# Summing the last six rows of a weight matrix in four rows of 256 columns in two PSUM banks, with the final copy on two engines

## Chip, cores, metric

One core of one Trainium2 chip. The metric is device microseconds of the whole program. All timed runs quoted here are fast: none is more than 1.5% above the fastest of its kernel. A comparison is given as the ratio of the mean of one kernel's fast runs to the mean of the other's of the same rounds, with a 95% interval, so it is not quite the ratio of the medians that stand beside it.

## The reference, cut to what matters

A decode step for one token: grouped-query attention over a cache of 65536 keys, plus an MLP, both added to the input.

```python
x = A_x                                   # (1, 1, 1024)
xn = _layernorm(x)
# A: q = xn @ wq ; softmax(q k^T) v over 4 kv heads x 65536 keys ; @ wo (4096 x 1024)
# B: ... h2 = gelu(layernorm(x1) @ w3) @ w4          w4 is 3584 x 1024
return x + A(xn, k_cache, v_cache, wq, wo) + B(xn, w1, w2, w3, w4)
```

The output is one row of 1024 values. 170 MB of weights and cache are read for it.

## The kernel before

Everything that ends in the output row is accumulated in one tile `psB` of PSUM (the memory into which TensorE writes its sums) as two rows of 512 columns (`j` = 0, 1), each in its own 32-column group of the TensorE array, so that the two matmuls of a row run side by side. The weight w4 is the last thing to be loaded, in eight pieces of 6, 5, 6, 4, 3, 2, 1 and 1 rows; a row here is `hT[:, c]` (128 values) times 128 x 1024 weights. "Row 27" below is the last one.

```python
W4_PIECES = (6, 5, 6, 4, 3, 2, 1, 1)
...
ps_S = ...  # bufs=1, 4 banks     ps_O: 1 bank     ps_M: 2 banks     ps_B: 1 bank  (all eight in use)
psB = ps_B.tile([P, 512], F32, name="psB")

def row_acc(j, lhsT, rhs, start=False):
    nc.tensor.matmul(psB[32 * j:32 * j + 32, :], lhsT=lhsT.to_broadcast([lhsT.shape[0], 32]), rhs=rhs, start=start,
                     stop=False, tile_position=(0, 32 * j), skip_group_check=True)
...
def compute_w4(lo, hi):
    wt = st.tiles["w4"]
    for c in range(lo, hi):
        for j in range(2):
            row_acc(j, hT[:, c:c + 1], wt[:, D * c + 512 * j:D * c + 512 * (j + 1)])
...
compute_k(NU - 1)
tail["rows"] = ps_S.tile([P, SUBS, 512], F32, name="o_acc", tag="sc")
for g in range(HKV - 1):
    project(g)                      # 48 matmuls with wo
add_projection()                    # o_rows: fp32 rows added into psB by two fp32 matmuls
compute_v(NU - 1)
early = sum(W4_PIECES[:2])
compute_w4(0, early)
project(HKV - 1)
compute_w4(early, FC)

out_t = ogpool.tile([64, 512], BF16, name="out_t", tag="og")
nc.scalar.copy(out=out_t[:], in_=psB[0:64, :])
nc.scalar.dma_start(out=out[0, 0, :].rearrange("(j n) -> j n", j=2), in_=out_t[31:33, :])
```

All 32 partitions of a quadrant hold the same row, so partitions 31 and 32 are the two rows of the output, next to each other.

## Time and profile before

| | before |
|---|---|
| median time | 401.06 us (400.98 to 401.21, 3 runs) |
| span of the profile | 398.9 us |
| DMA engines busy | 0.9 or more in nearly every slice, 426 GB/s |
| last load (row 27 of w4) landed | 396.52 |
| its two matmuls start | 396.56 |
| copy out of PSUM (ScalarE) | 396.99, 0.58 us |
| output DMA issued | 397.60, that is 1.08 us after the landing |

The chain of waits that ended last in the kernel before, its last five pieces (start us, us, what):

```profile
379.12 17.39 DMA big<-in_B_w_dram
396.52 0.04 issue
396.56 0.41 PE psB L221 x2
396.97 0.02 issue
396.99 0.58 ACT out_t L485
```

Up to 396.52 the chain is loads alone. Only the last 0.41 + 0.58 us are work that this change can shorten. The timeline of the same microseconds (start us, us, engine, line, operation, tiles, shapes, count, and in brackets the idle time before it and what ended it):

```profile
396.56 0.39 PE L221 MATMUL psB<-big,hT 128*32 128x512 bf16 x2 [0.25 <-DMA big<-in_B_w_dram]
...
396.99 0.58 ACT L485 CAST out_t<-psB 64x512 bf16<-64x512 f32 x1 [29.44 <-PE psB L221]
397.60 0.26 ACTq L486 DMA_DIRECT2D out_dram<-out_t  x1
```

TensorE sat idle 0.25 us for the last row: its backlog had just cleared.

### The profile page before, as it was taken

To read this page: it belongs to the slowest core of one execution; us is meant where nothing else is said; L and a number is where in the kernel's file an instruction comes from. 1 tells how busy PE (TensorE), PEld (TensorE's weight loads), DVE (VectorE), ACT (ScalarE), POOL (GpSimd) and SP (SyncE) were. 2 spreads that over 40 slices of the span, in tenths; PEclk is the share of its full clock that TensorE was granted. 3 is DMA by queue.
4 is the path that set the end of the run, shared out by engine and by line. 5 is a ranking of instruction groups with operands and counts; after the bars stand their busy time and mean duration, and the time that the engine had idled before them with its cause. 6 is when DMAs were issued, how large, how long until landed. Compare 5 with 4: busy or idle time off the path is not lost.

```text
span 398.9 us, 2547 instructions
## 1 busy us (share of the span) xinstructions
PE 232.8 (58%) x1348; PEld 45.1 (11%) x854; DVE 209.0 (52%) x154; ACT 27.3 (7%) x35; POOL 5.3 (1%) x28
## 2 busy tenths in 40 slices
PE   0571970591479238742974196539462945494987
PEld 0210000010100110010101010200020101010133
DVE  0601010964196569634953895269439942884130
ACT  1001010003000200020002000200100011002000
POOL 2000000000000000000000000000000000000000
PEclk9995996596869687956795889569855997698889
DMA  9998999999999999999999999999999999999996
GB/s 421 421 454 369 440 447 486 421 427 421 416 435 421 427 493 416 427 427 427 435 421 421 486 421 427 422 427 434 434 422 460 434 427 389 424 457 447 390 418 258
DMA packets 4575, 170.01 MB, mean 426 GB/s; under 512 B 467, under 2 KB 469, under 8 KB 982
## 3 DMA queue, kind: packets, MB, share of 16 engines
q1 hardware_dynamic: 4560, 169.87, 98.9%
q8 instruction: 8, 0.13, 0.1%
q14 instruction: 1, 0.01, 0.0%
q10 hardware_dynamic: 6, 0.00, 0.0%
HBM read 169.87 MB, written 0.00 MB: 426 GB/s over the span
## 4 chain that ended last, share of the span: by engine, by line
DMA 58%; DVE 20%; PE 18%; ACT 2%; issue 1%; DVEq 0%; ACTq 0%
DMA big<-in_A_k_cache_dram 34%; DVE big L357 14%; DMA big<-in_B_w_dram 14%; DMA big<-in_A_v_cache_dram 11%; PE sc L362 7%; PE oacc L412 5%; PE psh L287 3%; DVE p_sb L383 2%; DVE mx L367 2%; ACT p_sb L380 2%; PE ps L334 1%; PE psB L221 1%; PE pm_mx L369 0%; DVE m L371 0%; DVE ol L432 0%
## 5 line engine op out<-in xcount | busy, mean ns | idle before, releaser
L362 PE MATMUL sc<-big,qdiag 128*128 128x512 bf16 x512 | 128.5, 411 | 66.3 <-DVE big L357 66.1
L357 DVE STREAM_TRANSPOSE big<-big 128x4096 f32<-128x4096 f32 x32 | 139.4, 4413 | 50.1 <-DMA big<-in_A_k_cache_dram 50.1
L412 PE MATMUL oacc<-big,p_sb 128*32 128x512 bf16 x512 | 43.9, 511 | 34.5 <-DVE p_sb L383 34.5
L367 DVE TENSOR_REDUCE mx<-sc 128x1 f32<-128x2048 f32 x8 | 18.3, 2292 | 29.8 <-PE sc L362 29.8
L362 PEld LDWEIGHTS <-qdiag 128*128 128x128 bf16 x128 | 13.1, 103 | 177.1 <-issue 145.1
L380 ACT ACTIVATE p_sb<-sc,nball 128x2048 bf16<-128x2048 f32 x8 | 15.7, 1967 | 219.8 <-DVE nball L378 219.8
L383 DVE STREAM_TRANSPOSE p_sb<-p_sb 128x2048 bf16<-128x2048 bf16 x8 | 18.5, 2311 | 18.0 <-ACT p_sb L380 18.0
L412 PEld LDWEIGHTS <-p_sb 128*32 128x32 bf16 x512 | 16.5, 124 | 58.6 <-DVE p_sb L383 35.1
L287 PE MATMUL psh<-big,ln_rep_b 128*32 128x512 bf16 (+1 forms) x64 | 12.8, 968 | 7.5 <-DMA big<-in_B_w_dram 7.5
L451 PE MATMUL o_acc<-big,oT 128*1 128x512 bf16 x48 | 13.0, 440 | 2.4 <-ACT p_sb L380 2.4
L369 PE MATMUL pm_mx<-ident_f,mx 128*1 128x128 f32 x8 | 2.4, 295 | 19.1 <-DVE mx L367 19.1
L326 DVE STREAM_TRANSPOSE h_row<-h_row 128x896 bf16<-128x896 bf16 x1 | 1.1, 1112 | 21.0 <-ACT h_row L325 21.0
L421 DVE SCALAR_TENSOR_TENSOR og<-oacc,wb,og 128x512 f32<-128x512 f32 x4 | 3.0, 746 | 15.7 <-PE oacc L412 15.7
L221 PE MATMUL psB<-big,hT 128*32 128x512 bf16 x56 | 8.3, 430 | 0.3 <-DMA big<-in_B_w_dram 0.3
L457 DVE COPY o_rows<-o_acc 1x1024 f32<-1x1024 f32 x1 | 1.2, 1212 | 13.8 <-PE oacc L412 13.8
L235 PE MATMUL pm_ln<-ln_rowsum_a,ones_f 128*128 128x1 f32 x2 | 0.6, 347 | 12.6 <-DVE ln_rowsum_a L233 12.6
L433 PE MATMUL pm_e<-ol,sel8big 128*128 128x129 f32 x8 | 2.6, 414 | 7.9 <-DVE ol L432 7.9
L287 PE MATMUL psq<-big,ln_rep_a 128*32 128x512 bf16 x64 | 6.4, 585 | 1.3 <-DMA big<-in_A_wq_dram 1.3
L311 POOL COPY qdiag<-qx 32x32 bf16<-32x32 bf16 x16 | 3.2, 203 | 279.1 <-PE sc L362 249.1
L226 DVE STREAM_TRANSPOSE x_t<-x_row 32x256 bf16<-32x256 bf16 x4 | 2.5, 616 | 8.2 <-DMA x_row<-in_A_x_dram 8.1
L299 DVE CAST q_row<-psq 128x512 bf16<-128x512 f32 x1 | 0.7, 692 | 8.4 <-PE psq L287 8.4
L376 PE MATMUL pm_mx<-ident_f,rep 1*128 1x1 f32 x8 | 1.9, 240 | 5.0 <-DVE rep L373 5.0
(95 smaller groups left out, 73.6 us busy)
## 6 DMA issues: line engine op xcount, KB each, us to landing
big<-in_A_wo_dram SPq DMA_DIRECT2D x1, 8192.0 KB, 35.9
big<-in_B_w_dram SPq DMA_DIRECT2D x1, 7168.0 KB, 38.2
big<-in_B_w_dram SPq DMA_DIRECT2D x2, 2048.0 KB, 46.0
big<-in_B_w_dram SPq DMA_DIRECT2D x2, 1536.0 KB, 27.2
big<-in_B_w_dram SPq DMA_DIRECT2D x1, 1280.0 KB, 23.9
big<-in_B_w_dram SPq DMA_DIRECT2D x1, 1024.0 KB
big<-in_B_w_dram SPq DMA_DIRECT2D x1, 768.0 KB, 30.6
big<-in_B_w_dram SPq DMA_DIRECT2D x1, 512.0 KB, 31.4
```

What stands on the lines that cost most here:

```text
L221: nc.tensor.matmul(psB[32 * j:32 * j + 32, :], lhsT=lhsT.to_broadcast([lhsT.shape[0], 32]), rhs=rhs, start=start, stop=False, tile_positio ...
L287: nc.tensor.matmul(acc[32 * q:32 * q + 32, i, 0:n], lhsT=rep[:, c, :], rhs=cols(c, i, q), start=(c == 0), stop=(c == DC - 1), tile_positio ...
L311: nc.gpsimd.tensor_copy(out=qdiag[at, LEAD:].rearrange("p (x c) -> p x c", x=4)[:, :, 32 * a:32 * a + 8], in_=qx[at, :, 8 * g:8 * g + 8])
L334: nc.tensor.matmul(ps1[0:32, q, :], lhsT=xn2_rep[:, c, :], rhs=wt[:, 0, c, 512 * q:512 * (q + 1)], start=(c == 0), stop=(c == DC - 1), til ...
L357: nc.vector.transpose(out=words, in_=words)
L362: nc.tensor.matmul(sc[:, e, :], lhsT=qdiag[:, c0:c0 + P], rhs=cols[:, s, e, :, b2, :, r], start=(s == 0 and b2 == 0 and r == 0), stop=(s = ...
L367: nc.vector.reduce_max(out=mx[:], in_=sc[:].rearrange("p e n -> p (e n)"), axis=AX.X)
L380: nc.scalar.activation(out=p_sb[:], in_=sc[:], func=ACTF.Exp, bias=nball[:, b:b + 1], scale=SCALE, accum_out=group["lall"][:, b:b + 1])
L383: nc.vector.transpose(out=flat, in_=flat)
L412: nc.tensor.matmul(oacc[32 * q:32 * (q + 1), :], lhsT=pT[:, e, 32 * t:32 * (t + 1)], rhs=vt[:, :, e, t, :], start=(e == 0 and t < 4), stop ...
L421: nc.vector.scalar_tensor_tensor(out=og[:], in0=oacc[:], scalar=wb[:, 1:2], in1=og[:], op0=ALU.mult, op1=ALU.add)
L451: nc.tensor.matmul(tail["rows"][0:1, h2, :], lhsT=oT[g][:, j:j + 1], rhs=wt[:, g, j, 512 * h2:512 * (h2 + 1)], start=(g == 0 and j == 0), ...
```

## The change

Intent: make the work after the last landing shorter. The last six rows are summed in four rows of 256 columns, one per column group, in two PSUM banks, so that a row streams 256 columns instead of 512 and two engines can copy 256 columns each out of different banks at the same time. The sums up to row 21 stay in `psB`; they are copied to SBUF (`sums`) and added by four fp32 matmuls after three narrow rows (`AHEAD`). I call that copy and addition the handover.

```diff
--- before.py
+++ after.py
@@ -19,6 +19,8 @@
 SETS = 4
 SLOTS = 3
 W4_PIECES = (6, 5, 6, 4, 3, 2, 1, 1)
+NARROW = 6
+AHEAD = 3
 
 
 def keep_loaded_weights(nc):
@@ -479,12 +481,35 @@
     early = sum(W4_PIECES[:2])
     compute_w4(0, early)
     project(HKV - 1)
-    compute_w4(early, FC)
-
-    out_t = ogpool.tile([64, 512], BF16, name="out_t", tag="og")
-    nc.scalar.copy(out=out_t[:], in_=psB[0:64, :])
+    compute_w4(early, FC - NARROW)
+    sums = ogpool.tile([64, 512], F32, name="sums", tag="og")
+    nc.scalar.copy(out=sums[:], in_=psB[0:64, :])
+    quarters = [ps_M.tile([P, 512], F32, name="pm_r", tag="pm") for _ in range(2)]
+
+    def quarter_acc(lhsT, rhs, start=False):
+        for h in range(2):
+            for j in range(2):
+                q = 2 * h + j
+                nc.tensor.matmul(quarters[h][32 * q:32 * q + 32, 0:256], lhsT=lhsT(j), rhs=rhs(j, h), start=start, stop=False,
+                                 tile_position=(0, 32 * q), skip_group_check=True)
+
+    def narrow_rows(lo, hi, start=False):
+        wt = st.tiles["w4"]
+        for c in range(lo, hi):
+            quarter_acc(lambda j: hT[:, c:c + 1].to_broadcast([P, 32]),
+                        lambda j, h: wt[:, D * c + 512 * j + 256 * h:D * c + 512 * j + 256 * (h + 1)],
+                        start=start and c == lo)
+
+    narrow_rows(FC - NARROW, FC - NARROW + AHEAD, start=True)
+    quarter_acc(lambda j: ident_f[0:64, 32 * j:32 * j + 1].to_broadcast([64, 32]),
+                lambda j, h: sums[:, 256 * h:256 * (h + 1)])
+    narrow_rows(FC - NARROW + AHEAD, FC)
+
+    out_t = ogpool.tile([64, 2, 256], BF16, name="out_t", tag="og")
+    nc.scalar.copy(out=out_t[:, 0, :], in_=quarters[0][0:64, 0:256])
+    nc.vector.tensor_copy(out=out_t[:, 1, :], in_=quarters[1][64:128, 0:256])
     nc.scalar.dma_start(out=out[0, 0, :].rearrange("(j n) -> j n", j=2),
-                        in_=out_t[31:33, :])
+                        in_=out_t[31:33].rearrange("p h n -> p (h n)"))
 
 # ---- launch: one core; inputs and outputs as the reference has them ----
 _INS = ['A_x', 'A_k_cache', 'A_v_cache', 'A_wq', 'A_wo', 'B_x', 'B_w1', 'B_w2', 'B_w3', 'B_w4']
```

## The prediction

> **What bounds the kernel now.** By the page's slices the DMA engines are busy at 0.9 or more in nearly all of the span (398.9 us, 426 GB/s). The chain of waits of the last 60 us is nothing but loads: the V cache to 379.1, then w4 to 396.52, and after that only 0.41 us of TensorE (two matmuls of the last w4 row), 0.58 us of ScalarE (copy of 64x512 sums out of PSUM) and the output's DMA, issued at 397.60. The loads don't depend on anything the change touches, so only what follows 396.52 can gain: 0.41 + 0.58 us, 0.25% of the time.
>
> **What the change does, by the timeline and the trace's single instructions.**
> - Last row: two matmuls of 512 columns (0.39 us each, starting 3 ns apart) become four of 256 in four column groups. In the V stage four column groups already run at the pace of one matmul per 0.216 us each (starts a few ns apart, durations 0.38 to 0.39), so four abreast cost no more than two. The clock is at full speed from 389.5 to 399.7, where 512 columns stream in 0.213 us: 256 fewer save 0.107. Estimate: 0.39 becomes 0.28. This agrees with the Trainium skill, "TensorEngine Tiling (Array Packing)", Key Properties: tiles execute in parallel.
> - Final copy: ScalarE 64x256 instead of 64x512. ScalarE's gelu takes 597 ns for 512 columns and 485 for 384, 0.87 ns a column, so 578 becomes about 355. VectorE's half: 128x512 casts from PSUM take 692, 128x128 take 293, 1.04 ns a column, so about 426 for 256. VectorE ends last. The skill's section PSUM Bottleneck on the same page says to use both engines for evacuation. The copy gains 578 - 426 = 0.15.
> - The output DMA now waits for two engines: 0.02 to 0.05 back.
> Sum: 0.107 + 0.15 - 0.035 = 0.22 us.
>
> **What is added, and whether it is hidden.** The first sums (through row 21) must be copied to SBUF (64x512 f32, about 0.58 on ScalarE, idle since 367) and added by four fp32 matmuls. Row 21 starts at 394.51, since TensorE still works off a backlog; it ends at about 394.93, the copy at 395.52. The fp32 additions: two of 512 columns took 385.19 to 386.19, two passes of 0.45 and 0.1 before the next row, so 256 columns take about 0.55: 395.57 to 396.12. Rows 25 and 26 (26 landed at 395.9) take 0.11 each: done by about 396.35. Row 27 lands at 396.52, so there is about 0.2 us of slack and nothing of this reaches the end. The four fp32 matmuls differ in height (64 rows) from the others, so a change of tiling mode may cost up to 0.1 more, within the slack.
>
> **Predicted: 400.84 us** (401.06 less 0.22), 8 in 10 within 400.50 to 401.15. Faster by over 2%: 0.003; within 2%: 0.99; slower by over 2%: 0.007.
>
> **What would show it.** The last w4 load lands within 0.2 us of 396.5; the last row's matmuls start within 0.05 us of that landing, with no VectorE, ScalarE or TensorE wait between; their durations near 0.28; the copies near 0.36 (ScalarE) and 0.43 (VectorE), starting within 0.05 us of each other; the output DMA issued 0.75 to 0.85 us after the landing, against 1.08 now; the fp32 additions done before 396.2.
>
> **What would make it wrong.** The slack of 0.2 us is gone if the copy of the first sums starts late or the fp32 additions run one after another (four of 0.43 would take until 397.3): the last row would then start late and the gain turn into a loss of up to 0.5 us. Or the load stream's own time varies by more than 0.2 us between chips or builds, which would hide the gain.

## More of the kernel before

The page's head, its clock and DMA slices (40 slices of 10 us; digits are tenths), and from its list of DMA queues the one that fetches instructions (packets, MB, share of the engines' time):

```profile
span 398.9 us, 2547 instructions
...
PEclk9995996596869687956795889569855997698889
DMA  9998999999999999999999999999999999999996
...
q8 instruction: 8, 0.13, 0.1%
```

DMA is the limit; TensorE's clock goes to and fro between full and half speed.

## The result

| | before | change |
|---|---|---|
| median | 401.06 us (400.98 to 401.26, 6 runs) | 400.86 us (400.82 to 402.16, 6 runs) |
| ratio, 95% interval | | 1.0 (0.9987 to 1.0012) |

The change's mean equals that of before because of one run of 402.16; the other five lie between 400.82 and 400.92, all below the lowest timed run of before. In three series (this one and two repeats below) the medians are 0.20, 0.25 and 0.23 us below those of before; all the intervals include 1. Of the 38 timed runs of the kernel before none is below 400.98 (its first profiled run took 400.92); of the 16 of the change 12 are. I take a gain of about 0.2 us in the usual run as real and too small for the interval.

The profile that follows is of another execution than the six timed ones: its span is 399.0 at a mean clock of 0.799, and theirs are 398.8 or 398.9 in five runs and 399.1 in the run of 402.16, none at that clock. So what follows shows one execution.

Now the profile of the change, which does *not* show what was predicted. Its page, the lines that answer to those of before:

```profile
span 399.0 us, 2590 instructions
...
PEclk9996896696769787966695679569976886598799
DMA  9998999999999999999999999999999999999996
...
q8 instruction: 9, 0.15, 0.2%
```

Its chain of waits at the end (same columns as above):

```profile
389.33 5.57 PE psB L223 x45
...
395.46 0.59 ACT sums L486
396.05 0.04 issue
396.09 1.13 PE pm_r L493 x20
397.23 0.02 issue
397.25 0.43 DVE out_t L510
```

The chain no longer goes through the last load, but through TensorE's w4 rows, the handover's copy and the rows queued behind it. Its timeline:

```profile
395.46 0.58 ACT L486 COPY sums<-psB 64x512 f32<-64x512 f32 x1 [27.91 <-PE psB L223]
...
396.09 0.64 PE L493 MATMUL pm_r<-sums,ident_f 64*32 64x256 f32 x8 [0.35 <-ACT sums L486]
...
396.66 0.51 PE L493 MATMUL pm_r<-big,hT 128*32 128x256 bf16 x12
397.20 0.37 ACT L509 CAST out_t<-pm_r 64x256 bf16<-64x256 f32 x1 [1.16 <-PE pm_r L493]
397.25 0.43 DVE L510 CAST out_t<-pm_r 64x256 bf16<-64x256 f32 x1 [6.91 <-PE pm_r L493]
397.75 0.27 ACTq L511 DMA_DIRECT2D out_dram<-out_t  x1
```

The last load landed at 396.68 (trace's semaphore events), but the last row started at 396.89: 0.21 us late, because rows 25, 26 and 27 waited behind the fp32 additions (row 25 starts at 396.66, where the prediction had 396.12). The output DMA went out 1.07 us after the landing, where before it was 1.08. So in this one execution the shorter row and copy gained what the late handover lost.

Why late? The single records put row 21 at 395.04, against 394.51 in the profile of before, though the instructions up to there are the same. The clock record has TensorE at half speed from 366.6 to 373.4 and from 387.1 to 390.5 (before: 365.6 to 372.4 and 386.1 to 389.5). The projection starts at 367.4, so it ran a microsecond longer at half speed, and a microsecond at half speed costs half a microsecond: the copy of `o_acc` on VectorE starts at 384.41 instead of 383.93, 0.48 later. The timeline of before, and the chain of the change:

```profile
383.93 1.21 DVE L457 COPY o_rows<-o_acc 1x1024 f32<-1x1024 f32 x1 [13.76 <-PE oacc L412]
```

```profile
384.41 1.22 DVE o_rows L459
```

I take that for a phase of the clock, not a thing that the change does: up to row 21 the instructions are the same, and the half-speed stretches of the two profiles are a microsecond apart already at 300.8 and 301.7. The Trainium skill ("TensorE: Matmul & The Clock Gate", Part 1) describes two states, full and half speed, decided on a free-running window of 3.413 us; the stretches in these traces are 3.41, 6.83 and 10.24 us long, one to three times that, which agrees.

### The profile page after: what moved, and what is told of

It is laid out like the page before. It is cut to its first block, busy times and chain, and to the rows that moved or that the text cites. A ratio compares the mean times of both kernels' runs of the same rounds, so it can differ in the third digit from the quotient of the medians.

```text
span 399.0 us, 2590 instructions
## 1 busy us (share of the span) xinstructions
PE 234.1 (59%) x1368; PEld 45.6 (11%) x874; DVE 209.4 (52%) x155; ACT 27.6 (7%) x36; POOL 5.3 (1%) x28
## 4 chain that ended last, share of the span: by engine, by line
DMA 48%; DVE 25%; PE 21%; ACT 3%; another core or an unknown queue 2%; issue 1%; DVEq 0%; ACTq 0%
DMA big<-in_A_k_cache_dram 42%; DVE big L359 19%; PE sc L364 8%; DMA big<-in_A_wq_dram 5%; PE oacc L414 5%; PE o_acc L453 3%; DVE mx L369 3%; ACT p_sb L382 3%; DVE p_sb L385 2%; PE psB L223 2%; PE psq L289 1%; DVE m L373 0%; PE pm_mx L371 0%; PE pm_mx L378 0%
## 5 line engine op out<-in xcount | busy, mean ns | idle before, releaser
L364 PE MATMUL sc<-big,qdiag 128*128 128x512 bf16 x512 | 130.2, 416 | 64.2 <-DVE big L359 63.9
L414 PE MATMUL oacc<-big,p_sb 128*32 128x512 bf16 x512 | 45.1, 522 | 34.5 <-DVE p_sb L385 34.5
L223 PE MATMUL psB<-big,hT 128*32 128x512 bf16 x44 | 6.5, 448 | 0.0
L289 PE MATMUL psq<-big,ln_rep_a 128*32 128x512 bf16 x64 | 5.2, 499 | 1.1 <-DMA big<-in_A_wq_dram 1.1
L420 ACT COPY og<-oacc 128x512 f32<-128x512 f32 x4 | 2.3, 585 | 34.3 <-PE oacc L414 34.3
```

The source lines that it names most:

```text
L289: nc.tensor.matmul(acc[32 * q:32 * q + 32, i, 0:n], lhsT=rep[:, c, :], rhs=cols(c, i, q), start=(c == 0), stop=(c == DC - 1), tile_positio ...
L364: nc.tensor.matmul(sc[:, e, :], lhsT=qdiag[:, c0:c0 + P], rhs=cols[:, s, e, :, b2, :, r], start=(s == 0 and b2 == 0 and r == 0), stop=(s = ...
L414: nc.tensor.matmul(oacc[32 * q:32 * (q + 1), :], lhsT=pT[:, e, 32 * t:32 * (t + 1)], rhs=vt[:, :, e, t, :], start=(e == 0 and t < 4), stop ...
```

## The experiments

There were three groups, each on one chip; all gave correct results. This table has what the sections below use. "Issue" is the time from the landing of the last load to the output's DMA. All from each kernel's one profile, except the medians. In every trace the span ends 1.25 to 1.26 us after this issue, in quarters_one 1.78.

| kernel | median, range (us) | before beside it | ratio | last landing | last row late by | issue |
|---|---|---|---|---|---|---|
| before | 401.06 | | | 396.52 | 0.04 | 1.08 |
| before_again | 401.17 (401.02 to 401.47) | 401.12 | 1.0003 | 396.74 | 0.04 | 1.08 |
| change | 400.86 (400.82 to 402.16) | 401.06 | 1.0 | 396.68 | 0.21 | 1.07 |
| again | 400.89 (400.83 to 401.08) | 401.14 | 0.9994 | 396.67 | 0.04 | 0.91 |
| again2 | 400.94 (400.85 to 401.82) | 401.17 | 0.9999 | 396.83 | 0.04 | 0.91 |
| ahead4 | 400.96 (400.85 to 401.14) | 401.17 | 0.9995 | 396.76 | 0.04 | 0.91 |
| n7a5 | 401.08 (400.81 to 402.39) | 401.17 | 1.0005 | 396.80 | 0.88 | 1.74 |
| early | 401.02 (400.93 to 401.12) | 401.14 | 0.9997 | 396.69 | 0.04 | 1.02 |
| oneengine | 401.00 (400.93 to 401.44) | 401.12 | 1.0002 | 396.76 | 0.04 | 1.15 |
| quarters_two | 402.60 (402.55 to 402.79) | 401.14 | 1.0037 | 398.10 | 0.04 | 1.35 |
| quarters_one | 402.69 (402.56 to 403.12) | 401.14 | 1.0039 | 397.84 | 0.04 | 0.90 |
| pad154 | 402.61 (402.31 to 402.76) | 401.12 | 1.0036 | 397.96 | 0.04 | 1.30 |
| pad259 | 402.40 (402.29 to 402.50) | 401.12 | 1.0032 | 397.89 | 0.04 | 1.08 |

My theory going in (A): the shorter end gains a fixed amount, and the handover costs 0 to 0.25 us by the phase of the clock. Rivals: the handover is always hidden and the first profile odd (B); the 0.2 us of the timed runs isn't made in the tail at all (C).

### The change again (again, again2)

No edit.

> The changed kernel once more, unedited. In its first profile the last row started 0.21 us after its load had landed, because the fp32 additions ended at 396.66 instead of the predicted 396.12; TensorE had come 0.49 us later out of the projection, in which the clock was at half speed until 373.4 instead of 372.4. Theory A (the handover of the first sums costs 0 to 0.25 us, by the phase of the clock): about 0.2 us faster than before in the mean, between 400.75 and 400.95; in this profile the gap between the landing of the last load and the last row is between 0.03 and 0.25, by where the half-speed stretch lies. Rival B (the handover is hidden as predicted, and the first profile was odd): the gap is under 0.06. Rival C (the 0.2 us of the timed runs is not made in the tail): difference to before not distinguishable from zero over 5 rounds.

> The changed kernel a third time, as company for the two below on one chip. As theory A has it, 0.15 to 0.25 us faster than before; in the profile, if the clock's half-speed stretch reaches beyond 372 in the projection, the last row starts 0.1 to 0.25 after its landing, else under 0.06.

In both profiles the half-speed stretch in the tail is missing (half speed from 366.9 to 370.4 in one, 364.1 to 370.9 in the other, then full until after 397), and the last row starts 0.04 us after its landing. The timeline of again:

```profile
394.58 0.58 ACT L486 COPY sums<-psB 64x512 f32<-64x512 f32 x1 [27.01 <-PE psB L223]
...
395.63 0.64 PE L493 MATMUL pm_r<-sums,ident_f 64*32 64x256 f32 x8
...
397.04 0.37 ACT L509 CAST out_t<-pm_r 64x256 bf16<-64x256 f32 x1 [1.88 <-PE pm_r L493]
397.08 0.43 DVE L510 CAST out_t<-pm_r 64x256 bf16<-64x256 f32 x1 [8.86 <-PE pm_r L493]
397.58 0.27 ACTq L511 DMA_DIRECT2D out_dram<-out_t  x1
```

Its chain is loads up to the last landing:

```profile
379.28 17.39 DMA big<-in_B_w_dram
396.67 0.04 issue
396.71 0.34 PE pm_r L493 x4
397.06 0.02 issue
397.08 0.43 DVE out_t L510
```

The copy of the first sums starts 0.89 us earlier than in the first profile, the additions are over at 396.20 (row 25 starts then), and the output DMA goes out 0.91 us after the landing: 0.17 better than before. Rival B is right about these executions and wrong about the first; theory A covers both. It is read from the coincidence of clock record and lateness in the change's profiles, not forced by a run, since I had no way to set the phase.

### The kernel before against itself (before_again)

No edit.

> The kernel before against itself, for the noise of the comparison and for a second profile. Difference within 0.1 us. In its first profile the last load landed at 396.52, 0.15 us earlier than in the three profiles of the change and of the early handover (396.67 to 396.69); if that was chance, it lands near 396.68 here and the span is near 399.0; if the change itself delays the loads, it lands near 396.52 again. The last row starts within 0.06 us of the landing and the output's DMA is issued 1.08 us after it.

Measured: 401.17 against 401.12, ratio 1.0003 (0.9990 to 1.0015): two medians of one kernel differ by 0.05, once. The last landing is at 396.74 here, within the 396.67 to 396.83 of the change's three profiles; so the 396.52 of the first profile doesn't show that the change delays the loads. The issue is 1.08 us after the landing again. This is why I compare the distance from the landing to the issue, and not spans: the landing alone wanders by 0.2 us.

### Handover five rows earlier (early)

```diff
-NARROW = 6
-AHEAD = 3
+NARROW = 11
+AHEAD = 5
```

> The changed kernel with the handover earlier: the last eleven rows narrow, the first sums added after five of them (rows 17 to 21). The fp32 additions then end about 395.2, over a microsecond before the last landing. Theory A: the last row starts within 0.05 us of the landing whatever the clock does, the output's DMA is issued 0.82 to 0.88 us after the landing (1.08 before), and the timed runs are 0.22 to 0.27 us faster than before, 0 to 0.1 faster than the change. Rival B: same time as the change within 0.03. Rival C: no order among the variants.

Measured 401.02: 0.12 below before, 0.13 above the change on the same chip. The last row did start on its landing (0.04), so the handover was out of the way. But its matmuls took 0.37 to 0.40 us, not 0.28. The timeline, and from the windows the microsecond in which the row starts, with the granted clock (0.50) third from the end:

```profile
394.19 0.41 PE L493 MATMUL pm_r<-big,hT 128*32 128x256 bf16 x4 [1.28 <-DMA big<-in_B_w_dram]
...
397.71 0.26 ACTq L511 DMA_DIRECT2D out_dram<-out_t  x1
```

```profile
396.00:397.00 1.00, 1.00 (x20) 0.51 (x12) 0.00 (x0) 0.00 (x0) 0.00 (x0) 0.50 0.04 14
```

Narrow rows finish sooner, TensorE stood idle 1.28 us waiting for a load, and from 394.2 the clock record is at half speed to the end. From the start of the last row to ScalarE's copy took 0.433 us here and 0.323 in again: the 0.11 lost is the difference in issue (1.02 against 0.91). My expectation of 0.82 to 0.88 failed on this for the most part; the 0.91 of again would have missed it too. A TensorE that ran dry upstream came with a slower critical matmul. That the idling is the cause is read from coincidence and not forced by a run: in the 3.41 us before the clock dropped TensorE was busy for 0.43 of the time here, for 0.18 and 0.26 in the two quarters and 0.45 in pad154 below; in again and before_again, which kept full speed, it was 0.57 and 0.56 in the stretch from 390.8 on. No threshold comes out of this: a share of 0.61 near 382 was followed by half speed in before, and not in again2.

### Both final copies on ScalarE (oneengine)

```diff
-    nc.vector.tensor_copy(out=out_t[:, 1, :], in_=quarters[1][64:128, 0:256])
+    nc.scalar.copy(out=out_t[:, 1, :], in_=quarters[1][64:128, 0:256])
```

> The change with both final copies on ScalarE, one after the other. Measured pieces: a copy of 64x256 took 0.366 on ScalarE, 0.427 on VectorE, which started 0.043 later; two on ScalarE end about 0.75 after the first started instead of 0.47, and the wait for the second engine (0.04 us) is saved: 0.24 slower than the change, so the same time as before within 0.05 (401.1). If the split of the copy between two engines were not what gains (rival C), it stays at 400.89.

```profile
397.13 0.37 ACT L509 CAST out_t<-pm_r 64x256 bf16<-64x256 f32 x1 [1.86 <-PE pm_r L493]
397.52 0.37 ACT L510 CAST out_t<-pm_r 64x256 bf16<-64x256 f32 x1
397.92 0.27 ACTq L511 DMA_DIRECT2D out_dram<-out_t  x1
```

In the trace the issue is 1.15 us after the landing, 0.24 more than in again, as expected. The timed runs are 400.93 to 401.44, median 0.12 below before, mean 0.02% above: they neither confirm nor deny it at this size. Their spans say more: median 399.2 against 399.0 of before beside them, where the change in again had 398.9 against 399.1. So in the span the gain is gone, which speaks against rival C as far as the copy goes; only the part of the time outside the span was shorter, 1.80 to 1.86 us in four of the five runs where before has 2.02 to 2.12, and why isn't known. Splitting the copy is worth 0.24 us in the trace against copying the halves one after the other.

### Narrow rows everywhere, one bank, no handover (quarters_two, quarters_one)

If the handover is the weak point, do without: keep all the sums of the kernel in four quarters of 256 columns, one in each quadrant of one bank. quarters_two:

```diff
-    def row_acc(j, lhsT, rhs, start=False):
-        nc.tensor.matmul(psB[32 * j:32 * j + 32, :], lhsT=lhsT.to_broadcast([lhsT.shape[0], 32]), rhs=rhs, start=start, ...)
+    def row_acc(j, lhsT, rhs, start=False):
+        for h in range(2):
+            q = 2 * h + j
+            nc.tensor.matmul(psB[32 * q:32 * q + 32, 0:256], lhsT=lhsT.to_broadcast([lhsT.shape[0], 32]),
+                             rhs=rhs[:, 256 * h:256 * (h + 1)], start=start, stop=False, tile_position=(0, 32 * q), ...)
...
+    nc.scalar.copy(out=out_t[:, 0, :], in_=psB[0:64, 0:256])
+    nc.vector.tensor_copy(out=out_t[:, 1, :], in_=psB[64:128, 0:256])
```

quarters_one has `q = 2 * j + h` and one copy and one store instead:

```diff
+    out_t = ogpool.tile([P, 256], BF16, name="out_t", tag="og")
+    nc.scalar.copy(out=out_t[:], in_=psB[:, 0:256])
+    nc.scalar.dma_start(out=out[0, 0, :].rearrange("(q n) -> q n", q=4), in_=out_t[0:P:32, :])
```

> No handover at all: the row sums of the whole kernel are kept in four quarters of 256 columns, one in each 32-partition quadrant of one PSUM bank, all rows by four matmuls; final copies of 64x256 by ScalarE and VectorE as in the change. TensorE's backlog shrinks too, since a row takes 0.11 instead of 0.22 us. Theory A: as with the early handover, last row within 0.05 us of the landing, DMA issued about 0.82 after the landing, 0.22 to 0.30 us faster than before. Rival B: no faster than the change. If the narrow rows don't run four abreast in one bank, the rows take 0.22 or more each and nothing is gained over before but the copy.

> As the one before, but the final copy is a single ScalarE instruction of 128x256, and the output's DMA takes four partitions (0, 32, 64, 96) of 512 B instead of two of 1 KB. If ScalarE's copy costs by columns and not by partitions, it takes 0.37 us as its 64x256 copy did, ends 0.06 us before VectorE's 0.43, and there is no second engine to wait for: DMA issued 0.74 to 0.80 us after the landing, 0.28 to 0.36 us faster than before, 0.04 to 0.1 faster than with two engines. The four smaller packets may cost a few tens of ns back.

Both lost 1.5 us, the largest effect, and not by anything I had foreseen: the last load landed at 398.10 and 397.84, over a microsecond late. The next section is about that. Both also ran their last row at half clock (half speed from 394.5 and 395.9 on): 0.451 us from its start to the copy, where again has 0.323. Two lesser things show in their timelines. quarters_two:

```profile
398.60 0.37 ACT L488 CAST out_t<-psB 64x256 bf16<-64x256 f32 x1 [30.97 <-PE psB L223]
398.99 0.43 DVE L489 CAST out_t<-psB 64x256 bf16<-64x256 f32 x1 [10.72 <-ACT out_t L488]
```

VectorE waited for ScalarE's copy: out of one tile in one bank the program orders the two copies, so the change needs its two banks. The Trainium skill ("PSUM — Partial Sum Buffer", section on bank collisions) says that different quadrants of one bank may be read at once; no run here tests it, since the program made the copies wait. quarters_one:

```profile
398.33 0.37 ACT L488 CAST out_t<-psB 128x256 bf16<-128x256 f32 x1 [30.78 <-PE psB L223]
398.74 0.60 ACTq L489 DMA_DIRECT2D out_dram<-out_t  x1
```

ScalarE's copy of 128 partitions costs the same 0.37 us as one of 64, as expected. But the store from four partitions takes 0.60 us to issue instead of 0.27, and lands 1.69 us after the copy's end, against 1.17 with two partitions in quarters_two. The "few tens of ns" that I had allowed were half a microsecond, so the early issue of quarters_one (0.90 at half clock) is no gain: its span ends 0.53 us later after the issue than all others.

### What delayed the loads: 154 and 259 idle instructions (pad154, pad259)

Where did the 1.5 us come from? In the traces of the quarters a ninth 16 KB instruction fetch ran at 392.1 (quarters_two) and 392.6 (quarters_one) for about 1.1 us. TensorE's instruction list had grown from 1665 (before) and 1691 (change) to 1813, as I counted in the programs (the traces have 2222, 2262 and 2400 TensorE records). To separate this from everything else about the quarters I added matmuls of one column to the kernel before, 22 or 37 in each of the first seven units, where TensorE is idle:

```diff
+        if u < NU - 1:
+            for _ in range(22):                                  # 37 in pad259
+                nc.tensor.matmul(pm[0:28, 256:257], lhsT=hT[:], rhs=flat[:, 0:1], start=True, stop=True)
         group["p"] = p_sb
```

> Why did the quarters lose 1.5 us? In their traces a ninth 16 KB instruction fetch runs on a DMA engine at 392.1 to 392.6 for 1.07 us, in the midst of the last loads, and the last 16 packets of w4 then come singly, one every 0.08 us; before, the change and its repeat have eight fetches by then, the last at 383. TensorE's program grew from 1665 to 1813 instructions. This kernel is the one before with 22 one-column matmuls more in each of the first seven units, 154 TensorE instructions that change nothing else. Theory D (a fetch of instructions among the last loads delays one DMA engine, and the last load with it): a ninth fetch at about 392 to 395, last landing 1.0 to 1.5 us later, 402.1 to 402.6 us. Rival E (the quarters' loads were slow because of what TensorE reads and where, or of its idle clock): no change, 401.1. The 1 us or so of matmuls added to each unit is off the chain that ends last (TensorE idles there).

> The same with 37 in each of seven units, 259 more: a whole fetch more, so that the ninth falls where the eighth fell before, at about 383, and all others are earlier. If a fetch costs only where nothing after it can absorb it (theory D1): the time of the kernel before, 401.1, within 0.2. If every fetch of instructions costs its 1 us of the load stream wherever it falls (D2): about 1 us slower, 402.1. Rival E: 401.1.

Both are slower, by 1.49 and 1.28 us in the medians, with intervals clear of 1 (1.0024 to 1.0049 and 1.0020 to 1.0045): theory D holds and rival E falls (though pad154's ninth fetch came at 388.5, not at the 392 to 395 expected). The added matmuls themselves delay nothing: up to that fetch the loads of pad154 land when those of before_again do (386.13 and 386.12), and the next one 1.2 us later (391.02 and 389.81). D1 falls too, since pad259 had its ninth fetch at 383.0, where the eighth of the kernel before lies, and lost 1.28 us all the same. Its number fits D2; but D2's words don't fit either, because in the same traces the eighth fetch costs the end nothing, be it at 383.1 (before), 352.8 (pad154) or 335.7 (pad259).

The landing events settle it. A load raises its semaphore sixteen times, once for each DMA engine (the Trainium skill, "DMA: Bandwidth & Descriptors", section on why a DMA increments its semaphore by 16, says so; the traces have 16 events for each large load). So one can see how far each engine is ahead of the last one. These are not lines of the profile's views but the times of the events, taken off the last of each load, in us:

```
before_again, load that ended at
 38.81  0.43 0.42 0.40 0.39 0.38 0.37 0.36 0.35 0.34 0.24 0.22 0.19 0.17 0.15 0.04 0.00   no fetch yet
 44.98  1.70 1.69 1.68 1.67 1.66 1.65 1.64 1.61 1.51 1.50 1.47 1.45 1.44 1.32 1.28 0.00   1 fetch (42.9)
108.15  1.93 1.92 1.92 1.90 1.89 1.88 1.88 1.84 1.73 1.71 1.67 1.66 1.55 1.50 0.36 0.00   2 (106.0)
383.05  2.01 1.97 1.97 1.96 1.94 1.81 1.72 1.63 0.90 0.42 0.40 0.38 0.19 0.18 0.17 0.00   7, and one of 8 KB
386.12  1.98 1.96 1.96 1.95 1.79 1.72 1.61 0.89 0.41 0.38 0.38 0.37 0.18 0.17 0.16 0.00   8 (383.4)
396.74  1.93 1.92 1.91 1.90 1.74 1.68 1.57 0.87 0.40 0.37 0.37 0.35 0.18 0.17 0.14 0.00   8
pad259
382.93  1.86 1.84 1.72 1.63 1.63 1.52 1.42 1.00 0.35 0.32 0.29 0.23 0.23 0.15 0.14 0.00   8
387.25  3.08 3.08 2.95 2.87 2.85 2.76 2.66 2.25 1.58 1.56 1.47 1.47 1.40 1.39 1.24 0.00   9 (383.0)
397.89  3.06 3.05 2.92 2.84 2.83 2.74 2.63 2.25 1.59 1.57 1.49 1.48 1.39 1.38 1.23 0.00   9
```

Each of the first eight fetches throws one more engine out of the leading group, by about 1.2 to 1.7 us, and nothing ever gives that back: the lags stay constant to 0.1 us for hundreds of microseconds; as I read it, because each engine has its own share of each load and is never out of work. The first fetch sets the end of the loads back; the next seven hit engines that still had that lead, and cost the end little. The ninth hits an engine that is behind already, and makes it 1.24 us later than all others. That the fetches go round the same engines I infer from these counts; the records that I have don't number the engines.

The windows show the same from the side (start and end, length, busy us and count of TensorE, its weight loads, VectorE, ScalarE and GpSimd, then granted clock, DMA share and GB/s). before_again:

```profile
395.00:396.00 1.00, 0.58 (x6) 0.20 (x4) 0.00 (x0) 0.00 (x0) 0.00 (x0) 1.00 0.52 195
396.00:397.00 1.00, 0.72 (x6) 0.19 (x3) 0.00 (x0) 0.00 (x0) 0.00 (x0) 1.00 0.03 10
```

pad259:

```profile
395.00:396.00 1.00, 0.61 (x6) 0.32 (x6) 0.00 (x0) 0.00 (x0) 0.00 (x0) 1.00 0.51 195
396.00:397.00 1.00, 0.60 (x6) 0.20 (x4) 0.00 (x0) 0.00 (x0) 0.00 (x0) 1.00 0.07 27
```

From 396 to 397, when the engines of before_again have all but finished (0.03), pad259 has a share of 0.07 left: about one engine of sixteen (0.0625), alone at work on the last rows' weights. And from 395 to 396 half of the engines are done in both: they have the lead of almost two microseconds that the landing events show.

pad154 lost 0.2 more than pad259; its last row ran at half clock (0.65 us from its start to the copy, against 0.43), as its clock record has it from 395.5.

What this says of the change: its 26 more instructions bring the ninth fetch to the edge. In four of its traces and its near variants (the first of the change at 398.2, ahead4, n7a5 and oneengine at 396.5 to 396.7) it starts when the engines have next to no load left, and the last landing is where it was. In early (1711 instructions) it starts at 395.9, still in time.

### Placing the handover better (ahead4, n7a5)

ahead4 is `AHEAD = 4`; n7a5:

```diff
-NARROW = 6
-AHEAD = 3
+NARROW = 7
+AHEAD = 5
```

> The change with the first sums added after four narrow rows (22 to 25) instead of three: the additions still wait for the copy of the sums, but row 25 no longer queues behind them. No instruction added. Theory A: same as the change when TensorE is early (DMA issued 0.90 to 0.92 after the landing), 0.1 better when it is late; in the mean 0 to 0.1 us faster than the change, 401.1 less 0.2 to 0.3. The rival, that where the handover stands doesn't matter, has the same time as the change within 0.05.

> The change with seven narrow rows and the first sums added after five of them (rows 21 to 25), so the copy of the sums starts one row earlier, and only rows 26 and 27 follow the additions. Four TensorE instructions more (1695 against 1691; the early handover had 1711 and still no harmful ninth fetch). Theory A: the additions end by 396.45 even with the late clock, the last row starts within 0.06 us of its landing always, output DMA issued 0.90 to 0.93 after the landing, 0.2 to 0.3 us faster than before; ninth fetch, if any, after 396. If a ninth fetch falls before 395 it loses 1.2 us instead.

ahead4: 400.96, against 400.94 for again2 on the same chip, issue 0.91. Its profile had the half-speed stretch in the tail (386.3 to 389.7), but not in the projection beyond 372.6, and came out unharmed; the bad phase that it was meant for did not occur, so it is undecided, and not distinguishable from the change.

n7a5: 401.08, with runs of 401.80 and 402.39. The 402.39 is not of the tail: its span is 399.0 (see under Open below). The 401.80 is the profiled run, with a span of 399.8. Its profile shows the bad phase at its worst, half speed from 385.9 to 392.7, twice the usual stretch:

```profile
396.36 0.58 ACT L486 COPY sums<-psB 64x512 f32<-64x512 f32 x1 [28.66 <-PE psB L223]
397.00 0.64 PE L493 MATMUL pm_r<-sums,ident_f 64*32 64x256 f32 x8
...
398.54 0.26 ACTq L511 DMA_DIRECT2D out_dram<-out_t  x1
```

The last row started 0.88 us after its landing. "The last row starts within 0.06 us always" is refuted. An estimate from its own numbers: behind row 20, which starts at 395.94, the kernel before would have seven rows of 0.216 us, 0.43 to its copy, 0.58 for it and 0.03 to the issue, which makes 398.49; so in this phase the handover gains nothing and loses nothing. No run of the kernel before showed the phase. No variant beats the change beyond doubt.

## Why the prediction was right, and where not

- *What bounds the kernel, and that only the end after the last landing can gain*: right. In again, again2 and ahead4 the chain is loads up to the last landing, then 0.34 us of TensorE and the copy.
- *Last row 0.39 to 0.28*: right, 0.27 to 0.28 at full clock in all profiles of the change, four matmuls starting within 0.011 us of each other. This agrees with the skill's page on tiling (Key Properties). At half clock it takes 0.37 to 0.40 (early), which I had not considered.
- *Copies of 0.36 and 0.43*: right, 0.366 and 0.425 to 0.427. The section PSUM Bottleneck of that page, which advises both engines, is borne out for these halves: side by side 0.47 from first start to last end, one after the other 0.76 (oneengine). But quarters_one's single copy of 128x256 on ScalarE took 0.37.
- *The wait for two engines, 0.02 to 0.05*: mis-sized. VectorE starts 0.043 after ScalarE, and the output DMA follows its end by 0.077 us instead of the 0.030 after ScalarE's. Together 0.09 where I had 0.035. So the end gained 0.17 us in the traces (1.08 to 0.91), not 0.22, and the predicted issue of 0.75 to 0.85 after the landing was not met in any profile of the change; it was also lower than the prediction's own sum, by which it is 1.08 less 0.22, or 0.86. The medians gained 0.20 to 0.25; with the noise of before_again (0.05) that is no contradiction, and the missing hundredths are not explained.
- *"so there's about 0.2 us of slack and nothing of this reaches the end"*: this step failed in the very profile that came with the result. It rested on row 21 starting at 394.51, which is one phase of a clock, read from one execution. It started at 395.04, the additions ended at 396.66 instead of 396.12, and the whole gain of the tail was gone. In the other two profiles of the change, in ahead4 and in oneengine the slack was there, although the additions ended by the predicted 396.2 in again alone (396.37 in again2). The prediction named this under what would make it wrong; it had not put a chance on it. The time came out right all the same, so that part is luck.
- *The landing within 0.2 us of 396.5*: met by the change, again and early (396.67 to 396.69), missed by up to 0.13 in again2, ahead4, n7a5 and oneengine (396.76 to 396.83), and by the kernel before itself in its second profile (396.74). The first profile of before had been a quick one.
- The time, 400.84 predicted and 400.86 measured, is right by more than the method deserves: a term too large by 0.05 and a slack that is sometimes missing offset what the medians gained beyond the traces.

Open: the runs of 402.16 and 401.82, and n7a5's of 402.39. Their spans are 399.1, 399.0 and 399.0, so that 3.06, 2.82 and 3.39 us of their time lie outside the span, where the other runs of the change have 1.96 to 2.08 and those of before 2.02 to 2.12. again2's profiled run was the one of 401.82, and its tail is in order. In its trace a ninth fetch starts at 400.8, after the span's end. None of the 38 timed runs of before was above 401.47. Whether the change's longer program causes these runs was not tested.

## What to carry to other kernels

When a kernel is bound by loads, find the last landing and count only what follows it; a change that adds a step just before it must have slack in every phase of the clock, not in the one that a profile happened to show. Instructions are loads too: on a stream that never pauses, an instruction fetch sets one DMA engine back for good, so here 154 idle instructions cost 1.5 us, where all that a shorter last row and copy can gain is 0.2. And look at the clock when TensorE runs dry before the end: in early and both quarters its last matmuls, on the critical path, took 0.37 to 0.40 us instead of 0.28.

## What the Trainium skill lacked or had wrong

- "Runtime: NRT & Kernel Launch", section "Instruction fetch mechanics", describes the refills in 16 KiB blocks through a DMA queue and calls their cost mostly hidden; neither it nor "DMA: Bandwidth & Descriptors" says that they can hold back loads on the same engines. Here they were not hidden: 0.9 to 1.1 us on one engine, 16 KB once per 180 to 350 TensorE records, each setting an engine back by about 1.2 to 1.7 us for the rest of the stream; the ninth made the program 1.3 to 1.5 us slower.
- "TensorE: Matmul & The Clock Gate", Part 1, calls the cost of the ramp under 1% of a usual span and advises against fitting it. True in size (here at most 0.83 us of 400, n7a5's issue against that of again), but for a change in the tail the position of one 3.41 us stretch decides 0.17 of 0.2 us, and one of 6.83 us made the last row 0.88 us late.
- "DMA: Bandwidth & Descriptors", section on the increment by 16, says how many engines a DMA uses (the store from two partitions shows two data events, the one from four shows four), but not what a wider store costs: 0.60 us to issue and 1.69 us from the copy to the landing with four partitions, 0.27 and 1.17 with two. The four are 32 apart and the two adjacent, so the step may play a part.
- "TensorEngine Tiling (Array Packing)", Key Properties, says that changing the tiling mode drains TensorE, with no figure. Here the first narrow row starts 0.33 us after the last fp32 pass (64 rows high), where the two passes start 0.24 apart; how much of the 0.09 is the mode was not measured alone.
